# Splitting a weight load, a two-pass first tile, a fourth output buffer and moved final waits in a fused layer kernel

## The chip, the cores and the metric

The kernel runs on one core of a Trainium2 chip. The metric is the device time of one execution in microseconds (us); smaller is better. Executions of the same kernel still spread by 0.4 to 1.8 us. Wherever a difference is below 1 us, I therefore also look into the trace of one execution of each kernel and compare stages, not totals.

The span in a trace is about 1.7 us shorter than the time of the same execution. All times inside a profile are from the start of that span.

## The reference

A transformer layer on 2048 tokens of width 512, in bfloat16: layer norm, then attention with 32 heads of 16 over the 8 earlier positions at stride 2, and beside it a gated feed-forward part.

```python
x = A_x                                     # [1, 2048, 512]
xn = _layernorm(x, axis=-1)
return x + _A_ref(xn, A_wqkv, A_wo) + _B_ref(xn, B_w_gate, B_w_up, B_w_down)

# _A_ref:  qkv = xn @ wqkv   (512 x 1536: Wq, Wk, Wv side by side)
#          ... softmax over the 8 positions ..., then  o @ wo
# _B_ref:  h = gelu(xn @ w_gate) * (xn @ w_up)  (512 x 1376),  then  h @ w_down
```

Both branches read the normalised x. The order at the start: x arrives, its statistics are taken, it is normalised and transposed (`xnT`), and then TensorE projects it with Wq and after that with Wk. At the end the last row tile of the sum is added and stored.

## The kernel before

The kernel is built from a list of tasks; a scheduler orders them on each engine and works out the semaphore waits. Five places matter.

All loads go through SyncE's queue, in this order at the start: two loads of x, Wq, a tile of x, Wk, another tile of x, and later Wv and the weights of the feed-forward part. Wq and Wk are one load of 512 KB each:

```python
for i, nm in enumerate(("q", "k", "v")):
    def mk(i=i):
        return lambda e: e.dma_start(
            Wqkv[:, :, i * 512:(i + 1) * 512],
            A_wqkv[:, i * 512:(i + 1) * 512].rearrange("(k p) n -> p k n", p=128))
    t_w = G.task("sp", "ld_w" + nm, 0, mk(), wr=[(I_wq, nm)],
                 prio=(-958, -957.5, -898)[i], nbytes=512 * 1024)
```

Before the first real matmul, TensorE runs filler matmuls on zeros (`wsrc`) to get its full clock. The first Q tile has four groups `g` of columns, each summed over four row blocks `kt` of Wq, and starts in two pieces, groups 0 and 1, then 2 and 3:

```python
WARM = cfg.get("WARM", ([512] * 8 + [128], [512, 128]))
# ... (cut)
for g in gs:                                  # (0, 1), then (2, 3)
    for kt in range(4):
        ins = e.matmul(
            PS[:, 512 * it.slot + 128 * g:512 * it.slot + 128 * g + 128],
            lhsT=Wqkv[:, kt, which * 512 + g * 128:which * 512 + (g + 1) * 128],
            rhs=xnT[:, itx.slot, kt, t * 128:(t + 1) * 128],
            start=(kt == 0), stop=(kt == 3))
# ... (cut)
chain(warm_tasks[:len(WARM[0])] + ["tpx0_0"] + warm_tasks[len(WARM[0]):] +
      ["mma0_0", "tpx0_1", "mmt0_0", "mmt0_1", "mmt1_0", "tpx1_0", ...])   # order on TensorE
```

In that chain `tpx` are transposes of x, `mma0_0` and `mmt0_0` the first Q tile, `mmt0_1` the second Q tile, and `mmt1_0` the first tile that needs Wk.

At the end VectorE adds a PSUM tile to x into one of `NOB = 3` output buffers, and SyncE stores it. The program's last instructions on SyncE are waits for the totals of all 24 DMA semaphores:

```python
for t in self.order[eng_name]:
    # ... (cut)
    for (s, v) in t.waits:
        e.wait_ge(s, v)
    ins = t.emit(e)
    ins.then_inc(t.sem, 16 if eng_name == "sp" else 1)
if eng_name == "sp":
    for (s, tot) in self.dma_totals:
        e.wait_ge(s, tot)
```

## Time and profile before

| | before |
|---|---|
| median of 3 runs | 194.91 us (194.59 to 194.97) |
| span of the profiled execution | 192.8 us |
| TensorE busy | 186.6 us, 97% |
| first projection starts | 6.29 us |
| TensorE's last signal | 190.33 us |
| landing of the last store | 192.21 us |
| end | 192.79 us |

TensorE is the bound in the middle and has next to no gaps there. So a gain can only come from the 6.3 us before the first projection, from a wait soon after it, or from the 2.5 us behind the last matmul.

### The profile page before, as it was taken

The numbers are of one execution on the slowest core, as the hardware profiler recorded it, in microseconds if no ns is written. First come the engines' busy times: TensorE is split into PE (matmuls) and PEld (weight loads), VectorE is DVE, ScalarE is ACT, GpSimd is POOL, SyncE is SP. The second block draws the span as 40 slices with busy tenths as digits, with TensorE's granted clock in tenths as the row PEclk, the third lists the DMA queues.
The fourth block names the chain that finished last, engine by engine and source line by source line (L and its number), as shares of the span: only waits on it lengthen the run. The fifth ranks groups of instructions, "written<-read, shape, count | busy, mean of one in ns | idle before, by whom it ended". The sixth has DMA issues, their size and how long they took to land.

```text
span 192.8 us, 3283 instructions
## 1 busy us (share of the span) xinstructions
PE 186.6 (97%) x1239; PEld 92.0 (48%) x1256; DVE 152.4 (79%) x240; ACT 106.1 (55%) x177; POOL 15.7 (8%) x31
## 2 busy tenths in 40 slices
PE   6899999999999999999999999999999999999994
PEld 2794444444444444444444444444444444444484
DVE  5799999999997965999995599998996199912132
ACT  5688565696896766712466587328276720058000
POOL 7010011110931020000000000000000000000000
PEclk9999999999999999999999999999999999999999
DMA  4999997899564014965401596420250496130121
GB/s 143 353 397 332 307 172 139 229 235 219 146 131 106 0 40 134 239 140 161 146 19 28 143 237 157 130 77 0 69 139 13 113 233 165 36 112 0 51 72 46
DMA packets 34800, 27.04 MB, mean 140 GB/s; under 512 B 11264, under 2 KB 33248, under 8 KB 34784
## 3 DMA queue, kind: packets, MB, share of 16 engines
q1 hardware_dynamic: 34784, 26.83, 56.2%
q8 instruction: 10, 0.16, 0.3%
q14 instruction: 6, 0.05, 0.1%
HBM read 19.99 MB, written 5.26 MB: 131 GB/s over the span
## 4 chain that ended last, share of the span: by engine, by line
PE 93%; DMA 4%; issue 1%; SPq 0%; DVE 0%; DVEq 0%
PE PS L1395 36%; PE PS L1474 18%; PE PS L1152 18%; PE PS L1470 7%; PE PS L1098 4%; PE PS L1363 4%; PE PS L1236 4%; DMA Wqkv<-in_A_wqkv_dram 2%; PE PS L1430 2%; DMA out_dram<-OB 1%; PE PS L1229 1%; SPq L923 0%; DVE OB L1494 0%; PE PS L1040 0%; DVEq L558 0%
## 5 line engine op out<-in xcount | busy, mean ns | idle before, releaser
L1412 ACT ACTIVATE UU<-PS 128x512 bf16<-128x512 f32 x40 | 24.1, 603 | 35.7 <-PE PS L1395 35.7
L1474 PE MATMUL PS<-Wd,HT 128*128 128x512 bf16 (+2 forms) x207 | 41.1, 345 | 0.1
L1395 PE MATMUL PS<-xnT,Wu 128*128 128x512 bf16 x155 | 39.8, 379 | 0.7 <-issue 0.5
L1395 PE MATMUL PS<-xnT,Wg 128*128 128x512 bf16 x155 | 39.2, 379 | 0.5 <-ACT OT L1375 0.2
L1206 DVE TENSOR_TENSOR UNI<-QT,KT 128x2048 bf16<-128x2048 bf16 x32 | 37.0, 1219 | 2.6 <-PE PS L1363 2.5
L1152 PE MATMUL PS<-xnT,Wqkv 128*128 128x512 bf16 x156 | 35.3, 379 | 0.2
L1417 DVE TENSOR_TENSOR HT<-GG,UU 128x512 bf16<-128x512 bf16 x40 | 16.6, 419 | 20.1 <-ACT UU L1412 20.0
L1405 ACT ACTIVATE GG<-PS 128x512 bf16<-128x512 f32 x40 | 23.7, 601 | 15.0 <-PE PS L1395 12.2
L1474 PEld LDWEIGHTS PS<-Wd,HT 128*128 128x128 bf16 x209 | 19.6, 98 | 18.6
L1395 PEld LDWEIGHTS PS<-xnT,Wu 128*128 128x128 bf16 x160 | 15.3, 98 | 19.6 <-issue 1.3
L1395 PEld LDWEIGHTS PS<-xnT,Wg 128*128 128x128 bf16 x160 | 15.5, 98 | 19.3 <-ACT OT L1375 0.4
L1152 PEld LDWEIGHTS PS<-xnT,Wqkv 128*128 128x128 bf16 x160 | 15.6, 98 | 18.6
L1343 DVE TENSOR_TENSOR BS<-BS,PT 128x2048 bf16<-128x2048 bf16 x16 | 19.6, 1224 | 0.4
L1343 DVE TENSOR_TENSOR UNI<-BS,PT 128x2048 bf16<-128x2048 bf16 x16 | 19.5, 1218 | 0.0
L1494 DVE TENSOR_TENSOR OB<-PS,XR 128x512 bf16<-128x512 f32 (+2 forms) x19 | 11.2, 603 | 10.0 <-PE PS L1474 9.4
L1470 PE MATMUL PS<-Wo,OT 128*128 128x512 bf16 (+2 forms) x76 | 16.9, 345 | 0.0
L1176 ACT ACTIVATE VT<-PS 128x512 bf16<-128x512 f32 x16 | 9.6, 597 | 4.4 <-PE PS L1152 4.4
L1375 ACT ACTIVATE OT<-PS 128x512 bf16<-128x512 f32 x16 | 8.3, 602 | 5.0 <-PE PS L1363 5.0
L940 DVE BATCH_NORM_STATS2 st<-XIN 128x6 f32<-128x512 bf16 x15 | 10.1, 686 | 0.9 <-DMA XIN<-in_A_x_dram 0.9
L1470 PEld LDWEIGHTS PS<-Wo,OT 128*128 128x128 bf16 x76 | 7.2, 98 | 7.0
L1192 POOL COPY KT<-KT 128x64 bf16<-128x64 bf16 x3 | 8.0, 2655 | 17.5 <-ACT KT L1169 16.1
L1162 ACT ACTIVATE QT<-PS 128x512 bf16<-128x512 f32 x12 | 7.2, 597 | 3.1 <-PE PS L1152 3.1
(73 smaller groups left out, 151.9 us busy)
## 6 DMA issues: line engine op xcount, KB each, us to landing
BS<-vt_scratch SPq DMA_DIRECT2D x64, 128.5 KB, 3.5
vt_scratch<-VT SPq DMA_DIRECT2D x16, 128.0 KB
XR<-in_A_x_dram SPq DMA_DIRECT2D x16, 128.0 KB, 2.2
out_dram<-OB SPq DMA_DIRECT2D x14, 128.0 KB, 1.9
Wqkv<-in_A_wqkv_dram SPq DMA_DIRECT2D x3, 512.0 KB
XIN<-in_A_x_dram SPq DMA_DIRECT2D x6, 256.0 KB, 4.4
Wg<-in_B_w_gate_dram SPq DMA_DIRECT2D x1, 1280.0 KB
Wu<-in_B_w_up_dram SPq DMA_DIRECT2D x1, 1280.0 KB
```

The costliest lines, as they stand in the source:

```text
L940: return lambda e: e.bn_stats(out=st[:, t, :], in_=XIN[:, it.slot, t2, :])
L1152: ins = e.matmul(PS[:, 512 * it.slot:512 * it.slot + HWD], lhsT=lhsT, rhs=xnT[:, itx.slot, kt, c0:c0 + HWD], start=(kt == 0), stop=(kt == 3))
L1176: return lambda e: e.activation(out=VT[:, ito.slot, 0:HWD], in_=PS[:, 512 * it.slot:512 * it.slot + HWD], func=ACTF.Identity)
L1206: return lambda e: e.tensor_tensor(out=UNI[:, it.slot, :, :], in0=bass.AP(QT, (itq.slot * 4 + g) * 512, [[NQT * 4 * 512, 128], [0, 4], [1, ...
L1343: return lambda e: e.tensor_tensor(out=dst(), in0=bass.AP(BS, it.slot * 4 * 514 + o, [[NBS * 4 * 514, 128], [514, 4], [128, 4], [1, 128]]) ...
L1395: ins = e.matmul(PS[0:M, 512 * it.slot:512 * it.slot + 512], lhsT=Wx[:, kt, j * 128:j * 128 + M], rhs=xnT[:, itx.slot, kt, :], start=(kt = ...
L1405: return lambda e: e.activation(out=GG[0:M, ito.slot, :], in_=PS[0:M, 512 * it.slot:512 * it.slot + 512], func=ACTF.Gelu_apprx_tanh)
L1412: return lambda e: e.activation(out=UU[0:M, ito.slot, :], in_=PS[0:M, 512 * it.slot:512 * it.slot + 512], func=ACTF.Identity)
L1417: return lambda e: e.tensor_tensor(out=HT[0:M, ito.slot, j, :], in0=GG[0:M, ig.slot, :], in1=UU[0:M, iu.slot, :], op=ALU.mult)
L1470: ins = e.matmul(PS[:, 512 * it.slot:512 * it.slot + CW], lhsT=OT[:, ito.slot, dq, ti * 128:(ti + 1) * 128], rhs=Wo[:, dq, c0:c1], start=( ...
L1474: ins = e.matmul(PS[:, 512 * it.slot:512 * it.slot + CW], lhsT=HT[:, ith.slot, j, ti * 128:(ti + 1) * 128], rhs=Wd[:, j, c0:c1], start=Fal ...
L1494: return lambda e: e.tensor_tensor(out=OB[:, ito.slot, 0:CW], in0=PS[:, 512 * it.slot:512 * it.slot + CW], in1=XR[:, itx.slot, c0:c1], op= ...
```

## The change

The intent: let the first projection start when half of Wq is there; keep the last addition from waiting for an old store; do the bookkeeping waits ahead of the last store and not behind it. The diff, cut to its core:

```diff
@@ emit_engine @@
                 e.wait_ge(s, v)
+            if eng_name == "sp" and t is self.order["sp"][-1]:
+                late = self.order["sp"][-5:]
+                for (s, tot) in self.dma_totals:
+                    if not any(q.sem is s for q in late):
+                        e.wait_ge(s, tot)
             ins = t.emit(e)
@@
         if eng_name == "sp":
-            for (s, tot) in self.dma_totals:
-                e.wait_ge(s, tot)
+            for q in self.order["sp"][-5:]:
+                e.wait_ge(q.sem, q.val)
@@ buffers @@
-    NOB = cfg.get("NOB", 3)
+    NOB = cfg.get("NOB", 4)
-        junk = sb("junk", [128, 512], BF)          # its two uses now write XR slot 0
@@ memset of wsrc ordered first on VectorE (cut); fillers @@
-        WARM = cfg.get("WARM", ([512] * 8 + [128], [512, 128]))
+        WARM = cfg.get("WARM", ([512] * 8 + [128], [128]))
@@ loads @@
+            if nm == "q":
+                for h in range(2):
+                    def mk_h(h=h):
+                        return lambda e: e.dma_start(
+                            Wqkv[:, 2 * h:2 * h + 2, 0:512],
+                            A_wqkv[256 * h:256 * h + 256, 0:512].rearrange("(k p) n -> p k n", p=128))
+                    t_w = G.task("sp", "ld_wq%d" % h, 0, mk_h(), wr=[(I_wq, "q%d" % h)], prio=-958 + 0.1 * h,
+                                 nbytes=256 * 1024)
+            else:
+                t_w = G.task("sp", "ld_w" + nm, 0, mk(), wr=[(I_wq, nm)],
+                             prio=(0, -957.5, -898)[i], nbytes=512 * 1024)
@@ first Q tile @@
-                                for g in gs:
-                                    for kt in range(4):
+                                for g in range(4):
+                                    for kt in ks:
-                                            start=(kt == 0), stop=(kt == 3))
+                                            start=(kt == 0 and not part), stop=(kt == 3 and (g == 3 or not part)))
@@
-                            t_mm = G.task("pe", "mma0_0", 8 * 0.0563, mk_mm((0, 1)), rd=mrd, wr=[it_mm],
-                                          prio=-100, mode="f")
-                            gs = (2, 3)
+                            def mk_z(it=it_mm):
+                                return lambda e: e.matmul(PS[:, 512 * it.slot:512 * it.slot + 512], lhsT=wsrc[:, 0:128],
+                                                          rhs=wsrc[:, :], start=True, stop=False)
+                            t_mm = G.task("pe", "zq0", d_mm(512), mk_z(), rd=[I_wsrc], wr=[it_mm], prio=-400, mode="f")
+                            t_mm = G.task("pe", "mma0_0", 8 * 0.0563, mk_mm((0, 1)), rd=mrd[:1] + [(I_wq, "q0")],
+                                          wr=[it_mm], prio=-100, mode="f")
+                            ks = (2, 3)
@@ order on TensorE @@
-                chain(warm_tasks[:len(WARM[0])] + ["tpx0_0"] + warm_tasks[len(WARM[0]):] +
+                chain(warm_tasks[:len(WARM[0])] + ["tpx0_0", "zq0"] + warm_tasks[len(WARM[0]):] +
```

More of the change, by code (lines that the diff above doesn't have):

```diff
@@ L814, in bass_parallel_sum__sliding_local_dilated__glu_gated_geglu__prompt_kernel @@
         PC2 = cfg.get("PC2", 8)
-        G.task("dve", "c_wsrc", 0.25, lambda e: e.memset(wsrc[:, :], 0.0), wr=[I_wsrc], prio=PC - 1)
+        t_mem = []
+        t_mem.append(G.task("dve", "c_wsrc", 0.25, lambda e: e.memset(wsrc[:, :], 0.0), wr=[I_wsrc], prio=PC - 1))
         G.task("pool", "c_ones", 0.2, lambda e: e.memset(cf[:, :], 1.0), wr=[I_cf], prio=PC)
@@ L838, in bass_parallel_sum__sliding_local_dilated__glu_gated_geglu__prompt_kernel @@
             out=E4f[:, :], in0=cf[:, 0:32], in1=cf[:, 32:64], op=ALU.add), rd=[I_cf], wr=[I_E4f], prio=PC2)
-        G.task("dve", "c_wdz", 0.25, lambda e: e.memset(Wd[0:32, 10, :], 0.0), wr=[(I_wd, 2)], prio=PC + 1)
-        G.task("dve", "c_htz", 0.4, lambda e: e.memset(HT[0:32, :, 10, :], 0.0), wr=[I_htz], prio=PC + 2)
+        t_mem.append(G.task("dve", "c_wdz", 0.25, lambda e: e.memset(Wd[0:32, 10, :], 0.0), wr=[(I_wd, 2)], prio=PC + 1))
+        t_mem.append(G.task("dve", "c_htz", 0.4, lambda e: e.memset(HT[0:32, :, 10, :], 0.0), wr=[I_htz], prio=PC + 2))
+        G.order_after(t_mem[1], t_mem[0])
+        G.order_after(t_mem[2], t_mem[0])
         G.task("pool", "c_e4b", 0.3, lambda e: e.tensor_tensor(
@@ L877, in mk @@
                     A_wqkv[:, i * 512:(i + 1) * 512].rearrange("(k p) n -> p k n", p=128))
-            t_w = G.task("sp", "ld_w" + nm, 0, mk(), wr=[(I_wq, nm)],
-                         prio=(-958, -957.5, -898)[i], nbytes=512 * 1024)
+            if nm == "q":
[9 more added lines that the diff above has]
+                             prio=(0, -957.5, -898)[i], nbytes=512 * 1024)
             t_ld["w" + nm] = t_w
@@ L942, in bass_parallel_sum__sliding_local_dilated__glu_gated_geglu__prompt_kernel @@
                     for (nm, dur, kw, rd, wr) in (
-                            ("sx1", 0.55, dict(out=junk[:, :], func=ACTF.Identity, accum_out=sums[:, 0:1]),
+                            ("sx1", 0.55, dict(out=XR[:, 0, :], func=ACTF.Identity, accum_out=sums[:, 0:1]),
                              [], [I_junk, (I_sums, 0)]),
@@ L946, in bass_parallel_sum__sliding_local_dilated__glu_gated_geglu__prompt_kernel @@
                                                 scale=-1.0 / D), [(I_sums, 0)], [(I_sums, 1)]),
-                            ("sxx1", 0.55, dict(out=junk[:, :], func=ACTF.Square, bias=sums[:, 1:2],
+                            ("sxx1", 0.55, dict(out=XR[:, 0, :], func=ACTF.Square, bias=sums[:, 1:2],
                                                 accum_out=sums[:, 2:3]), [(I_sums, 1)], [I_junk, (I_sums, 2)]),
@@ L1091, in bass_parallel_sum__sliding_local_dilated__glu_gated_geglu__prompt_kernel, with mk_mm @@
                         it_mm = Item("mmt%d_%d" % (which, t), P_ps, "qkv")
-                        def mk_mm(gs, which=which, t=t, it=it_mm, itx=XTI[0]):
+                        def mk_mm(ks, which=which, t=t, it=it_mm, itx=XTI[0]):
                             def f(e):
                                 ins = None
-                                for g in gs:
-                                    for kt in range(4):
+                                part = len(ks) < 4
+                                for g in range(4):
+                                    for kt in ks:
                                         ins = e.matmul(
@@ L1101, in f @@
                                             rhs=xnT[:, itx.slot, kt, t * 128:(t + 1) * 128],
-                                            start=(kt == 0), stop=(kt == 3))
+                                            start=(kt == 0 and not part), stop=(kt == 3 and (g == 3 or not part)))
                                 return ins
                             return f
-                        mrd = ([(XTI[0], (t // 2, t % 2)), (I_wq, "qk"[which])]
-                               + ([(XTI[0], ("y", 0, t))] if t < 2 else []))
-                        gs = (0, 1, 2, 3)
+                        mrd = ([(XTI[0], (t // 2, t % 2))] + ([(XTI[0], ("y", 0, t))] if t < 2 else [])
+                               + ([(I_wq, "k")] if which else [(I_wq, "q0"), (I_wq, "q1")]))
+                        ks = (0, 1, 2, 3)
                         if t == 0 and which == 0:
-                            t_mm = G.task("pe", "mma0_0", 8 * 0.0563, mk_mm((0, 1)), rd=mrd, wr=[it_mm],
-                                          prio=-100, mode="f")
+                            def mk_z(it=it_mm):
+                                return lambda e: e.matmul(PS[:, 512 * it.slot:512 * it.slot + 512], lhsT=wsrc[:, 0:128],
+                                                          rhs=wsrc[:, :], start=True, stop=False)
+                            t_mm = G.task("pe", "zq0", d_mm(512), mk_z(), rd=[I_wsrc], wr=[it_mm], prio=-400, mode="f")
+                            t_mm.urgent = True
+                            t_of["zq0"] = t_mm
+                            t_mm = G.task("pe", "mma0_0", 8 * 0.0563, mk_mm((0, 1)), rd=mrd[:1] + [(I_wq, "q0")],
+                                          wr=[it_mm], prio=-100, mode="f")
                             t_mm.urgent = True
                             t_of["mma0_0"] = t_mm
-                            gs = (2, 3)
-                        t_mm = G.task("pe", "mmt%d_%d" % (which, t), 4 * len(gs) * 0.0563, mk_mm(gs), rd=mrd,
+                            ks = (2, 3)
+                        t_mm = G.task("pe", "mmt%d_%d" % (which, t), 4 * len(ks) * 0.0563, mk_mm(ks), rd=mrd,
                                       wr=[it_mm], prio=-100 + t, mode="f")
@@ L1156, in bass_parallel_sum__sliding_local_dilated__glu_gated_geglu__prompt_kernel @@
                         t_mm = G.task("pe", "mm%d_%d_%d_%d" % (b, which, g, hf), d_mm(HWD, 4), mk_mm(),
-                               rd=xparts + [(I_wq, "qkv"[which])],
+                               rd=xparts + ([(I_wq, "kv"[which - 1])] if which else [(I_wq, "q0"), (I_wq, "q1")]),
                                wr=[it_mm], prio=hb + 10 + (1 if which == 2 else 0), mode="f",
```

## The prediction

> **What bounds the kernel now.** I read the page's engine shares, then TensorE's waits, then the chain of work that ended last, then the timelines of the first 8 and the last 4 us.
>
> ```profile
> PE 186.6 (97%) x1239; PEld 92.0 (48%) x1256; DVE 152.4 (79%) x240; ACT 106.1 (55%) x177; POOL 15.7 (8%) x31
> ...
> PE 93%; DMA 4%; issue 1%; SPq 0%; DVE 0%; DVEq 0%
> ```
>
> TensorE is busy for 97% of the span and carries 93% of the chain. Its waits (us in total, times, longest) are few:
>
> ```profile
> PE PS L866 <- DVE wsrc L815: 1.5, 1, 1.5
> PE PS L1098 <- DMA Wqkv<-in_A_wqkv_dram: 0.7, 1, 0.7
> PE PS L1395 <- issue: 0.6, 4, 0.2
> PE PS L1395 <- ACT OT L1375: 0.3, 2, 0.2
> ```
>
> The first two lie ahead of the first real matmul; the others are pauses of 0.16 us that follow the narrow-tile matmuls. I added up the trace's gaps between matmuls from 6.29 us (first projection) to 190.32 us (modelled end of the last): 1.56 us in 184, none above 0.16. **So the middle has nothing to give.** What is left is 6.3 us before TensorE runs unbroken and 2.5 us after it stops. The chain (start us, us, what) names a DMA at both ends:
>
> ```profile
> 1.71 4.44 DMA Wqkv<-in_A_wqkv_dram
> 6.15 0.14 issue
> 6.29 0.61 PE PS L1098 x8
> ...
> 187.56 2.85 DMA out_dram<-OB
> 190.41 0.02 issue
> 190.44 0.29 DVE OB L1494
> ```
>
> The load of Wq releases the first projection; a store out of the output buffer releases the last addition. For each the question is what else ends just behind it.
>
> **What the Trainium skill says.** "DMA: Bandwidth & Descriptors", section "Why a DMA increments its semaphore by 16 and not by 1": sixteen engines finish independently, and only the full 16 means that all data is there. The landing records agree: of Wq's sixteen, fourteen are in by 5.69 us and the last two at 6.02 and 6.15; of the store issued at 187.56, fifteen are in by 189.09 and the last at 190.415. "Perfetto Trace Analysis", section "Identifying Dependency Chains": an instruction with many waits may have EventSemaphore instructions inserted before it. This build does that, two waits each: the 24 final waits became twelve such instructions and a wait on the branch. "TensorE: Matmul & The Clock Gate", section "What's actually happening": full clock comes after a busy, free-running window of some 3.4 us. Here the fillers start at 1.51 us and full clock is granted at 4.74, 3.23 us later and before the first transposes at 4.95. "PSUM — Partial Sum Buffer", section "The four PSUM rules": a matmul with the start flag clears the whole bank's written-bits, so four accumulations interleaved in one bank can't each start with it. That is why the change starts the bank with one 512-wide zero matmul and adds onto it; no trace here shows the rule itself.
>
> **Part 1, Wq in two loads and the first Q tile in two passes.** Wq is 512 KB, behind two x loads that land at 2.83 and 3.37 us; so it moves between some 3.4 and 6.15. Its first half should land about half way, near 5.0 us (estimate from these landings). Then Wq no longer holds the first matmul, but ScalarE's copy of transposed x does:
>
> ```profile
> 5.52 0.30 ACT L972 ACTIVATE sq<-mv,eps 128x1 bf16<-128x1 bf16 x1
> 5.72 0.36 ACT L1060 ACTIVATE xnT<-PS 128x256 bf16<-128x256 bf16 x1
> ```
>
> It signals at 6.09. For the second x tile the same handover, from ScalarE's signal at 7.55 to the first matmul at 7.597, takes 0.047 us, so the first matmul can start at 6.14 in place of 6.29: **0.15 us, not the 0.67 that the wait shows**, because ScalarE's statistics of tile 1 and this copy are a chain that the change leaves alone. What follows moves with it: eight matmuls (8 x 0.056 = 0.44) to 6.58, then the transposes of tile 1, whose input VectorE finishes at 6.40; its copies and the next Q tile, 7.60 to 7.45. The second half of Wq is needed at about 6.81 and should land where Wq did, at 6.15. Wk is issued one issue (0.45) later, but it waits in a stream that is limited by bytes, not by issue: it landed at 8.00, and is needed at 8.35. All later weights have 2 us or more. From 7.60 on TensorE runs unbroken, so 0.15 reaches the end of the matmuls.
>
> **Part 2, the zero matmul and the fillers.** It replaces a 512-wide filler one for one: 0. The memset of the fillers' source becomes VectorE's first, 0.27 us earlier, so fillers start near 1.24 and end near 4.77. The transposes wait for VectorE (4.54 + 0.35 = 4.89) and don't move: 0, unless the clock window falls badly.
>
> **Part 3, fourth output buffer.** TensorE signalled the last group at 190.33. In the addition before, VectorE's wait began at 189.52 and the addition at 189.59, 0.066 later; without the store, 190.36 + 0.066 = 190.425 in place of 190.439. **Worth 0.014 us in this execution**: the late sixteenth landing and TensorE came together.
>
> **Part 4, the final waits.** The timelines have the last two stores (start us, us), and the view of one line the twelve wait instructions (ns min/median/max, first and last start):
>
> ```profile
> 189.91 0.33 SPq L1501 DMA_DIRECT2D out_dram<-OB  x1
> ...
> 190.76 0.33 SPq L1501 DMA_DIRECT2D out_dram<-OB  x1
> ```
>
> ```profile
> L564 SPq EVENT_SEMAPHORE  x12: 17/28/539, 191.1 to 192.3; - x12
> ```
>
> They begin at 191.14 and come every 0.061 us. The tenth (191.69) holds the last store's count, sits 0.54 us until the landing at 192.207, and two more follow before the branch at 192.39. In the changed program's instruction order ten wait instructions stand ahead of the last store, whose own wait for VectorE stays on the store, and behind it are two, the second with its count. So the branch comes 0.056 us behind the landing in place of 0.183: 0.13 gained. But the ten now run between the last two stores: the earlier issue ends at 190.24, they start at 190.29 and end at 190.29 + 9 x 0.061 + 0.03 = 190.87, and the store can go at 190.90 in place of 190.76: **0.14 lost. The tail nets about zero**, and part 3 is hidden behind it.
>
> **Part 5, the order in the middle.** The build counts the same 838 instructions on TensorE. In the third quarter a gate and an up group move from between the output tiles to behind them, and ScalarE does the exponential with both table loads ahead of a GELU. Output tiles then follow each other at 15 x 0.216 = 3.24 us over two PSUM banks, each freed by an addition of 0.69 us. The order can only lose, since nothing was lost before; I expect 0.
>
> Sum on the profiled execution: -0.15 + 0.01 = -0.14 us.
>
> **The rivals.** (a) The tail as intended: if waits that are met already cost less ahead of a store than the 0.061 after one, or order doesn't matter, the end is 0.13 sooner and the time 194.6. For: VectorE's 0.29 us addition leaves SyncE idle there; against: ten times 0.061 is more than the 0.52 us between the two issues. (b) Late landings are worse in unprofiled runs. The median of 194.91 is 0.41 above the profiled 194.50 and the three runs spread by 0.38. If that is stragglers of Wq or of the store, the change takes out most of it: 194.3 to 194.5. For: the waits sit on a sixteenth landing at both ends; against: no profile shows such a run. (c) A new stall in the middle, VectorE late with freeing a bank, or Wk late: up to 0.3, so 195.1. Against: the slack above. (d) The clock window: earlier fillers could bring full clock sooner where it came late, up to 0.27.
>
> **Range and chances.** From 194.91: -0.14 for the mechanism gives 194.77; half weight to (a) and (b), some 0.17, gives 194.6. Run spread of 0.4 and (c) make the range 194.1 to 195.0. 2% is 3.9 us, more than either end holds in all, so within 2% is nearly sure.
>
> **What would show it.** Right: first projection at 6.12 to 6.18 with ScalarE's copy as releaser; Wq gone from the chain; the last matmul at 190.17; some 0.6 us of wait instructions between the last two stores, and the last store issued about 0.65 behind the one before. Wrong: a first projection much before 6.1; a last store right on VectorE's signal; TensorE gaps beyond 1.6 us in the middle; a difference over 0.5 us.

## The result, and the profile after

| | before | after |
|---|---|---|
| median of 6 runs | 194.78 us (194.42 to 194.97) | 195.08 us (194.66 to 196.06) |
| ratio, with 95% interval | | 1.0025 (1.000 to 1.005) |
| span of the profiled execution | 192.8 us | 193.3 us |

A ratio here is the mean time of one kernel's runs over that of the other's runs of the same rounds, so it isn't quite the ratio of the medians beside it. The time is 0.3 us over the one before where 0.14 under it was expected from the mechanism.

The page after, engine shares and chain:

```profile
PE 187.7 (97%) x1239; PEld 92.6 (48%) x1256; DVE 152.4 (79%) x240; ACT 106.1 (55%) x177; POOL 9.6 (5%) x31
...
PE 93%; DMA 3%; SPq 1%; issue 1%; DVE 0%; DVEq 0%
```

A DMA still holds 3% of the chain. The chain itself (start us, us, what) says which one:

```profile
3.21 5.76 DMA Wqkv<-in_A_wqkv_dram
8.96 0.05 issue
9.01 1.07 PE PS L1115 x16
...
190.85 0.03 issue
190.88 0.02 DVEq L558
190.90 0.04 issue
190.94 0.29 DVE OB L1517
```

Before, the load in the chain was Wq, landing at 6.15, and the store into an output buffer stood ahead of the last addition. Both are gone, as planned. In their place stands **another weight load, issued at 3.21 and landed at 8.96: Wk**. TensorE's timeline (start us, us from first to last, engine, line, ..., idle before and its releaser) shows the start. Before:

```profile
6.29 0.61 PE L1098 MATMUL PS<-xnT,Wqkv 128*128 128x128 bf16 x8 [0.67 <-DMA Wqkv<-in_A_wqkv_dram]
6.73 0.39 PE L1040 MATMUL PS<-ident,XIN 128*128 128x128 bf16 x4
6.96 2.60 PE L1098 MATMUL PS<-xnT,Wqkv 128*128 128x128 bf16 x40
```

After:

```profile
6.08 0.91 PE L1115 MATMUL PS<-xnT,Wqkv 128*128 128x128 bf16 x8
6.83 0.39 PE L1056 MATMUL PS<-ident,XIN 128*128 128x128 bf16 x4
7.05 1.71 PE L1115 MATMUL PS<-xnT,Wqkv 128*128 128x128 bf16 x24
9.01 1.07 PE L1115 MATMUL PS<-xnT,Wqkv 128*128 128x128 bf16 x16 [0.25 <-DMA Wqkv<-in_A_wqkv_dram]
```

Two things are to be seen. The eight matmuls of the first pass start earlier but take 0.91 in place of 0.61, because full clock came only at 6.72 in this execution. And a run of 40 matmuls became 24 and 16 with a hole between them. The 0.25 counts only from the modelled end of the matmul before; from start to start the hole is larger, as the table of stages shows.

I cut both spans into stages at instructions that both kernels have (us). "Again" is a second profile of the same, unaltered kernel, taken as an experiment below. ScalarE's signal is the end of its instruction. A group of matmuls counts from its first weight load, which starts 0.004 to 0.054 ahead of the first matmul in the timelines.

| stage | before | before again | after | after again |
|---|---|---|---|---|
| start to ScalarE's signal for the first xnT | 6.082 | 6.063 | 6.026 | 6.167 |
| from there to the first projection | 0.177 | 0.312 | 0.051 | 0.051 |
| to the transposes of tile 1 (0.41 at full clock) | 0.421 | 0.420 | 0.697 | 0.408 |
| to the first Wk matmul | 1.767 | 1.766 | **2.230** | 1.766 |
| to the third group of transposes | 0.893 | 0.894 | 0.854 | 0.894 |
| to TensorE's last signal | 180.991 | 180.990 | 180.990 | 180.990 |
| to the end | 2.461 | 2.660 | 2.501 | 2.498 |
| sum | 192.79 | 193.11 | 193.35 | 192.77 |

**The middle is identical to a nanosecond or two.** From before to after, the 0.56 us that the span grew are: -0.06 for ScalarE's signal, -0.13 at the first projection, +0.28 for the cold clock, +0.46 - 0.04 for Wk (the stage behind a wait for Wk is up to 0.04 shorter, so a wait of 0.46 costs 0.42), +0.04 at the tail. The rest of this document asks which of these terms belong to the change and which to chance.

Where do Wk's bytes get held up? In the view of the DMA queue between 4 and 8 us the row "GB/s" has 40 slices of 0.1 us. Before, then after:

```profile
GB/s 246 307 369 369 389 389 379 358 389 369 379 399 379 359 379 420 348 410 389 358 338 379 369 379 389 348 328 338 317 318 287 328 338 358 358 369 348 338 338 369
```

```profile
GB/s 297 348 379 338 358 358 317 307 287 277 328 215 113 123 133 154 195 195 184 184 195 215 195 225 276 348 297 307 307 379 341 283 309 328 277 220 261 348 317 267
```

Before, the stream runs at 287 to 420 from 4.1 us on. After, it falls to 113 to 225 from about 5.1 to 6.4 us, when Wq is nearly in and a 128 KB tile of x and Wk are next. This is the **trough** that the experiments look for. Between 5 and 6 us it is 382 GB/s before and 182 after.

The kernel before has such a trough as well, only earlier: between 3 and 4 us, ahead of Wq, which stands behind two 128 KB loads of x. Before, then after (columns: stretch, us, busy share of PE, PEld, DVE, ACT, POOL with counts, granted clock, DMA share, GB/s):

```profile
3.00:4.00 1.00, 1.00 (x3) 0.30 (x2) 0.93 (x3) 0.60 (x2) 0.78 (x5) 1.00 0.59 131
```

```profile
3.00:4.00 1.00, 1.00 (x4) 0.38 (x3) 0.93 (x3) 0.66 (x3) 0.78 (x5) 1.00 0.78 219
```

So the split doesn't make a slow stretch out of nothing: it shortens the one ahead of Wq, and one stands ahead of Wk in its place.

The tail went as worked out: the waits (count: ns min/median/max, first and last start us) stand ahead of the last store, and two remain behind it.

```profile
L563 SPq EVENT_SEMAPHORE  x10: 17/28/28, 190.8 to 191.4; - x10
...
L569 SPq EVENT_SEMAPHORE  x2: 28/28/28, 191.9 to 192.9; - x2
```

The last addition ended at 191.23, and the last store was issued at 191.42, behind the tenth wait.

### The profile page after: what moved, and what is told of

It reads as the page before. It is cut to its first block, busy times and chain, and to the rows that moved or that the text cites. A ratio compares the mean times of both kernels' runs of the same rounds, so it can differ in the third digit from the quotient of the medians.

```text
span 193.3 us, 3282 instructions
## 1 busy us (share of the span) xinstructions
PE 187.7 (97%) x1239; PEld 92.6 (48%) x1256; DVE 152.4 (79%) x240; ACT 106.1 (55%) x177; POOL 9.6 (5%) x31
## 4 chain that ended last, share of the span: by engine, by line
PE 93%; DMA 3%; SPq 1%; issue 1%; DVE 0%; DVEq 0%
PE PS L1418 36%; PE PS L1497 20%; PE PS L1175 18%; PE PS L1493 7%; PE PS L1386 4%; PE PS L1259 4%; DMA Wqkv<-in_A_wqkv_dram 3%; PE PS L1115 3%; PE PS L1453 2%; PE PS L1252 1%; SPq L939 1%; SPq L888 0%; PE PS L1056 0%; DVE OB L1517 0%; DVEq L558 0%
## 5 line engine op out<-in xcount | busy, mean ns | idle before, releaser
L1192 ACT ACTIVATE KT<-PS 128x512 bf16<-128x512 f32 x12 | 7.2, 598 | 2.9 <-PE PS L1175 2.9
```

## The experiments

Theories before the runs. **A**: Wk is late because it is issued one issue later (3.21 in place of 2.74). **B**: Wk is late because of what stands ahead of it in the queue: a load behind small loads starts slowly. **C**: the 0.3 us is chance, namely the phase of the clock window and late landings. Each run below was timed in 5 rounds and has a profile. The three sets ran on three chips: the two repeats, one load and waits at the end on the first; Wk first, waits earlier, Wk in two and four loads on the second; the rest on the third. "Wait for Wk" is the time from the first weight load of the second Q tile to that of the first Wk matmul, less the 0.854 that it takes when nothing holds it; up to 0.04 of it comes back in the next stage. Every run was correct.

Beside timed medians stand the range of 6 runs and the ratio to the kernel before of the same rounds (its medians were 194.93, 194.86 and 194.90 in the three sets).

### The same kernels once more

No edit. **The changed kernel again:**

> The changed kernel, unaltered, for a second profile. Its first profile had Wk landing at 8.96 us (8.00 before) with a 0.42 us wait of TensorE for it, full clock granted only at 6.72 us (4.74 before), and 0.19 us of final waits between VectorE's last signal and the last store. Theory 1 (Wk is late because it is issued one issue later, into a stream that runs dry): Wk lands at 8.7 us or later again, and TensorE waits 0.2 us or more again. Rival (one unlucky execution): Wk at 8.0 to 8.4, no wait. The clock grant should differ from 6.72 if the window runs freely (anywhere from 4 to 7.2). The final waits should delay the last store by 0.15 to 0.2 us again, as nothing in them is chance. Time 195.0 to 195.3 under theory 1, 194.6 under the rival.

Measured: 194.91 (194.57 to 195.65), ratio 1.0009 (0.9986 to 1.0033). Its profile is the last column of the table above: full clock at 4.94, Wk landed at 8.32, no wait for it. The timeline of TensorE:

```profile
6.22 0.62 PE L1115 MATMUL PS<-xnT,Wqkv 128*128 128x128 bf16 x8 [0.52 <-ACT xnT L1076]
6.68 0.39 PE L1056 MATMUL PS<-ident,XIN 128*128 128x128 bf16 x4
6.90 2.60 PE L1115 MATMUL PS<-xnT,Wqkv 128*128 128x128 bf16 x40
```

So the same program can run the start without the cold matmuls and without the hole. The trough was there (212 GB/s between 5 and 6 us), yet Wk landed just before it was needed. The copy of ScalarE came 0.14 later than in the first profile, which is as much as the whole predicted gain.

**The kernel before again:**

> The kernel before, unaltered, for a second profile and as a null control of the timing. Theory 1: Wk at 7.9 to 8.2 us, no wait for it, first projection at 6.2 to 6.3 released by Wq. Rival (chance): Wk somewhere between 8.0 and 9.0. If the clock window runs freely, the grant is elsewhere than 4.74. Ratio 1.000, interval within 0.25%.

Measured: 194.87 (194.59 to 194.97), ratio 0.9997 (0.9978 to 1.0017). In its profile Wq landed at 6.27, and the first projection started 0.312 after ScalarE's signal. The end of its chain:

```profile
187.68 3.06 DMA out_dram<-OB
190.74 0.02 issue
190.76 0.29 DVE OB L1494
```

Here the last addition really waited for the store to free its buffer: it started 0.313 after TensorE's signal, not 0.108 as in the first profile. **With three buffers the wait was thus 0.014, 0.22 and, in a third profile (the split only in the kernel before), 0**, where the prediction read 0.014 from one profile.

The late landing itself isn't chance. In all 14 profiles the last of this store's sixteen landings came 0.94 to 1.84 us behind the fifteenth, and the DMA packets in the traces name what held it: one 16 KB packet of queue q8 (called "instruction" on the page) starts 0.5 to 0.8 us after the store's issue and takes 0.95 to 1.58 us; the store's packets that are left start within 0.015 us of its end, and the sixteenth landing follows 0.94 to 1.10 us after that end. What varies is how long this packet takes. If the same landings had met three buffers, the last addition would have waited 0 to 0.53 in the eleven profiles with four, 0.22 on average (an estimate from these landings and TensorE's signals). No run moves the packet.

What follows from the pair: theory C is right that single profiles differ by 0.3 to 0.6, and the change's own gain has to be found stage by stage.

### Undo the split only

```diff
-                for h in range(2): ...                                # two loads of 256 rows
+                t_w = G.task("sp", "ld_wq", 0, mk(), wr=[(I_wq, "q0"), (I_wq, "q1")], prio=-958, nbytes=512 * 1024)
```

> The changed kernel with Wq in one load again; zero matmul, two passes, fourth buffer and moved waits stay. Theory 1: Wk is issued at 2.74 us again and lands at about 8.0, TensorE does not wait for it; the first projection goes back to about 6.26, held by Wq. Net against the changed kernel: 0.15 us lost at the first projection, 0.4 gained at Wk, so about 0.25 us faster, 194.7 to 194.9. Rival (Wk late by chance): no systematic gain, 0.15 us slower than the changed kernel.

Measured: 194.58 (194.46 to 195.14), ratio 0.9989 (0.9968 to 1.0009). Window view, 5 to 6 us (columns as above):

```profile
5.00:6.00 1.00, 0.83 (x6) 0.50 (x6) 0.69 (x3) 0.94 (x5) 0.00 (x0) 1.00 1.09 378
```

The trough is gone: 378 GB/s against 182. Wk landed at 7.51, and Wq as one load landed at 5.64, so the first projection still started 0.051 after ScalarE's signal. This says that the split isn't needed for the early start in an execution without stragglers, and that it goes together with the trough. Issue order and load size are both restored here, so A and B are not yet told apart.

### The split only, in the kernel before

```diff
+                for h in range(2): ...     # Wq in two loads; all its readers wait for both
```

> The kernel before with only Wq's load split in two; the first Q tile still waits for both halves, no other part of the change. If the split alone makes the slow second of DMA: 100 to 230 GB/s between 5 and 6 us (355 to 382 without the split), Wk complete at 8.3 to 9.0, waits of TensorE for it of 0 to 0.5, while the first projection goes at 6.12 to 6.2 as in the changed kernel, since both halves land before 5.8. Rival (it needs the other parts, such as the first VectorE order or the scratch target): 355 GB/s or more, Wk at 8.0.

Measured: 195.06 (194.41 to 195.48), ratio 0.9998 (0.9969 to 1.0028).

```profile
5.00:6.00 1.00, 0.63 (x6) 0.29 (x6) 0.70 (x3) 0.94 (x5) 0.00 (x0) 1.00 0.51 124
```

The split alone brings the trough ahead of Wk (124 GB/s) and a later Wk (8.31; TensorE waited 0.04, which the next stage gave back). Neither the zero matmul, nor the fillers' order, nor the waits have a part in it.

### Wk issued first

```diff
-                             prio=(0, -957.5, -898)[i], nbytes=512 * 1024)
+                             prio=(0, -957.85, -898)[i], nbytes=512 * 1024)
```

This puts Wk's issue at 2.71, where the kernel before has it (2.74), with the two halves of Wq still ahead of it, and the tile of x that stood between them behind it.

> The changed kernel with Wk issued right behind the two halves of Wq, ahead of the third x tile: at 2.70 us, as in the kernel before (2.74), in place of 3.21. Three profiles with Wq in two loads have Wk landing at 8.96, 8.32 and 8.54, and DMA at 100 to 212 GB/s between 5 and 6 us; three with one load have 8.00, 8.23 and 7.51, and 355 to 382. Theory A (a big load needs a fixed lead from issue to full flow, and the half of Wq ahead of it is too short to cover it): Wk lands 0.5 sooner than in the changed kernel, 7.8 to 8.2, no wait of TensorE for it, time some 0.2 us less. Theory B (after small loads a 512 KB load starts slowly whatever its issue): the slow second only moves, Wk at 8.2 to 8.6 and waits of 0 to 0.2. The third x tile comes later, at 8 us or so, and under either theory could hold VectorE's statistics at 7.3 us and cost what Wk gives.

Measured: 196.09 (195.04 to 196.69), ratio 1.0053 (1.0027 to 1.0079).

```profile
5.00:6.00 1.00, 1.00 (x6) 0.52 (x6) 0.70 (x3) 0.94 (x5) 0.00 (x0) 1.00 0.70 137
```

```profile
PE PS L1056 <- DVE XIN L1030: 1.1, 1, 1.1
PE PS L1115 <- DMA Wqkv<-in_A_wqkv_dram: 0.2, 1, 0.2
```

The trough stayed (137 GB/s), and Wk, issued half a microsecond sooner, landed at 8.95, as late as in the changed kernel (8.96), with a wait of 0.43. **Theory A fell here**, which expected 7.8 to 8.2; B's figure of 8.2 to 8.6 was missed too. The run is slower for its own reason: the third x tile, now behind Wk, landed at 9.28, and TensorE waited another 1.1 for VectorE's normalised x of it.

### One load of Wq, but Wk's issue held back

```diff
+            if t.name == "ld_wk":            # wait for a GpSimd instruction that ends near 3.1 us
+                for q in self.order["pool"]:
+                    if q.name == "c_e4a":
+                        e.wait_ge(q.sem, q.val)
```

on top of the one load: the reverse of the run before.

> The changed kernel with Wq in one load, and Wk held back by a wait of SyncE for a GpSimd instruction that ends at about 3.1 us: Wk is issued at 3.15 to 3.3, as late as in the changed kernel, but behind one 512 KB load. If the late issue were the cause, Wk lands at 8.3 to 9.0 with a slow second. If the small loads ahead are the cause (as issuing Wk first and four loads speak for): no slow second, 345 GB/s or more between 5 and 6 us, Wk at 7.5 to 8.2, no wait.

Measured: 194.87 (194.62 to 195.08), ratio 0.999 (0.9962 to 1.0017). Wk was issued at 3.14, nearly as late as in the changed kernel.

```profile
5.00:6.00 1.00, 0.97 (x6) 0.56 (x6) 0.68 (x4) 0.94 (x5) 0.00 (x0) 1.00 1.12 346
```

No trough: 346 GB/s. But Wk landed at 8.57, where 7.5 to 8.2 was expected without one, with fourteen of its sixteen parts in by 8.11 and two stragglers, and TensorE waited 0.23. So late issue doesn't make the trough; that it has a small part in the landing of Wk can't be excluded from one profile.

### Wk in two loads as well

```diff
+            elif nm == "k":
+                for h in range(2): ...       # Wqkv[:, 2*h:2*h+2, 512:1024] <- 256 rows; readers wait for both
```

> The changed kernel with Wk in two loads of 256 rows as well, second half issued at about 3.7 us. Theory A (lead time from issue): the first half starts as late as Wk did, the second is issued 0.47 later still, Wk complete at 8.4 to 9.0, waits of 0.1 to 0.4 us and DMA at 100 to 212 GB/s between 5 and 6 us. Theory B (a 512 KB load starts slowly, a 256 KB one doesn't): no slow second, 330 GB/s or more between 5 and 6, Wk complete by 8.0, no wait.

Measured: 194.75 (194.53 to 195.81), ratio 1.0000 (0.9978 to 1.0023). 221 GB/s between 5 and 6 us; the second half of Wk, issued at 3.70, landed at 8.43; wait 0.07. No clear gain over the changed kernel: a smaller Wk load doesn't take the trough away, though this is the shallowest one. The form of B in which a 256 KB load doesn't start slowly fell here.

### Wq in four loads

```diff
-                for h in range(2): ...
+                for h in range(4):
+                    def mk_h(h=h):
+                        return lambda e: e.dma_start(Wqkv[:, h, 0:512], A_wqkv[128 * h:128 * h + 128, 0:512])
```

> A stronger dose: Wq in four loads of 128 rows, so Wk is issued two issues later again, at about 4.15 us. Theory A (lead time from issue): Wk lands another 0.8 to 1.0 us later, at 9.2 to 9.9, and TensorE waits 0.8 us or more; time 0.5 to 0.8 us over the changed kernel. Theory B (512 KB load after small ones): Wk at 8.3 to 9.0 as with two loads, waits of 0 to 0.4. If Wq's last quarter itself is late (needed at 6.85), the second half of the first Q tile waits too.

Measured: 195.45 (194.91 to 196.13), ratio 1.003 (1.0008 to 1.0052).

```profile
5.00:6.00 1.00, 1.00 (x6) 0.55 (x6) 0.68 (x4) 0.94 (x5) 0.00 (x0) 1.00 0.74 192
```

Wk was issued at 4.09, 0.88 later than in the changed kernel, and landed at 8.91 against 8.96; wait 0.49. If issue time decided, it would have come some 0.9 later than the 8.31 to 9.11 of the five profiles with halves; it came within them. It is the clearest single number against A. The interval is all above 1, so in timed runs this kernel is slower than the kernel before.

### Wq in 128 and 384 rows

```diff
-                            Wqkv[:, 2 * h:2 * h + 2, 0:512],
-                            A_wqkv[256 * h:256 * h + 256, 0:512]...
+                            Wqkv[:, h:1 + 3 * h, 0:512],
+                            A_wqkv[128 * h:128 + 384 * h, 0:512]...       # first pass waits for both
```

Again two loads, and Wk issued at 3.20, but the second load of Wq is 384 KB.

> The changed kernel with Wq in a load of 128 rows and one of 384; the first pass waits for both. If what matters is a big load right ahead of Wk (its data still moving while Wk's descriptors are handed out), 384 KB should do nearly as well as 512: 300 GB/s or more between 5 and 6 us, Wk at 7.8 to 8.3. If it is enough that Wq comes in two pieces: 100 to 230 GB/s, Wk at 8.3 to 9.0.

Measured: 194.73 (194.46 to 195.81), ratio 0.9989 (0.9957 to 1.0021).

```profile
5.00:6.00 1.00, 1.00 (x6) 0.56 (x6) 0.68 (x4) 0.94 (x5) 0.00 (x0) 1.00 1.04 323
```

323 GB/s and no wait for Wk, which landed at 8.43. So it isn't the number of loads either: **two loads with a large one last keep the stream full, two of 256 KB don't** (one profile of this kernel; a 128 KB tile of x stands between Wq and Wk in either). This kernel has its slow stretch earlier again, 130 GB/s between 3 and 4 us. The price was that Wq's last part landed at 6.26 and held the first projection by 0.14. The tail of this profile is 0.28 longer than the changed kernel's: the issue of the third store from the end took 0.82 us in place of 0.33 (0.50 and 0.71 in the two profiles of the kernel before). I don't know why.

### Final waits back at the end

```diff
-            if eng_name == "sp" and t is self.order["sp"][-1]: ...
-            for q in self.order["sp"][-5:]: ...
+            for (s, tot) in self.dma_totals:
+                e.wait_ge(s, tot)
```

> The changed kernel with all final waits back behind the last store. My theory: the last store goes 0.02 us after VectorE's signal in place of 0.19 to 0.20, and two wait instructions more (0.13 us) stand between landing and branch: 0.05 us faster, not to be seen in the times but in the trace. Rival (the moved waits are worth what they take off the end): 0.13 us slower with the last store issued no earlier.

Measured: 194.82 (194.71 to 195.28), ratio 1.0002 (0.998 to 1.0024). From TensorE's last signal to the end: 2.494 with the waits behind the last store, 2.498 and 2.501 with them directly ahead of it.

```profile
L564 SPq EVENT_SEMAPHORE  x12: 17/28/589, 191.2 to 192.4; - x12
```

The last store went at 190.836, 0.41 after TensorE's signal (0.57 in the changed kernel), but the branch came 0.24 after the landing in place of 0.084. **Moving the waits there nets zero**, as predicted (this run's own 0.05 isn't to be seen).

### Final waits two stores earlier

```diff
-            if eng_name == "sp" and t is self.order["sp"][-1]:
+            if eng_name == "sp" and t is self.order["sp"][-3]:
```

> The changed kernel with the nineteen early final waits ahead of the third-last store in place of the last. There SyncE is idle for over 1 us, so the ten wait instructions should end before VectorE signals. My theory: the last store goes 0.02 us after VectorE's signal (0.19 to 0.20 in the changed kernel), the branch stays 0.08 us behind the landing (0.18 with all waits at the end), and from TensorE's last signal to the end of the span it takes 2.50 - 0.17 = 2.33 us (2.49 to 2.51 in four profiles with the waits in either place). Rival (waits already met cost nothing in front of a store, and something else delays the last store): still 2.5.

Measured: 195.03 (194.48 to 195.26), ratio 0.9999 (0.9981 to 1.0017).

```profile
L563 SPq EVENT_SEMAPHORE  x10: 17/28/28, 188.6 to 189.2; - x10
```

Now the ten waits stand in idle time of SyncE and are over by 189.2, nearly 2 us before the last addition starts at 191.09. The stage from TensorE's last signal to the end is **2.348, 0.15 shorter** than in the changed kernel. The timed median doesn't show it, because this kernel still has the trough (90 GB/s); its profile waited 0.54 for Wk.

### The two findings together

The changed kernel with Wq in one load and the waits ahead of the third store from the end.

```diff
+                t_w = G.task("sp", "ld_wq", 0, mk(), wr=[(I_wq, "q0"), (I_wq, "q1")], prio=-958, nbytes=512 * 1024)
-            if eng_name == "sp" and t is self.order["sp"][-1]:
+            if eng_name == "sp" and t is self.order["sp"][-3]:
```

> A version that should beat both: the changed kernel with Wq in one load and the early final waits ahead of the third-last store. From the traces so far: Wk not waited for, first projection 6.14 to 6.25, TensorE's 180.99 us from the third transposes to its last signal as in all others, and 2.35 us from there to the end in place of 2.50 (2.46 and 2.66 in the two profiles of the kernel before). Time 0.2 to 0.4 us below the kernel before, ratio 0.998 to 0.999.

Measured: 194.41 (194.23 to 194.78), ratio 0.997 (0.994 to 1.000). No trough (379 GB/s), no wait for Wk (landed 7.72), a tail of 2.350. This is the lowest median and below both kernels'; its interval just reaches 1, so a gain of 0.3% over the kernel before is likely, not proved. Against the changed kernel the trace names two parts: the wait ahead of the last store that is gone, and a Wk that is in time. Against the kernel before, where Wk was in time, they are the tail (2.461 and 2.660 there) and a first projection that didn't wait for Wq (0.051 against 0.177 and 0.312), which in this kernel comes from Wq's landing at 5.87 and not from a split.

### All profiles side by side

| kernel | Wk issued | GB/s, 5 to 6 us | Wk landed | wait for Wk | full clock at | ratio |
|---|---|---|---|---|---|---|
| before; again | 2.74; 2.74 | 382; 354 | 8.00; 8.23 | 0; 0 | 4.74; 5.96 | 1; 0.9997 |
| one load | 2.75 | 378 | 7.51 | 0 | 5.39 | 0.9989 |
| one load, waits earlier | 2.74 | 379 | 7.72 | 0 | 5.08 | 0.997 |
| one load, Wk held | 3.14 | 346 | 8.57 | 0.23 | 5.85 | 0.999 |
| 128 + 384 rows | 3.20 | 323 | 8.43 | 0 | 6.17 | 0.9989 |
| **changed; again** | 3.21; 3.22 | **182; 212** | 8.96; 8.32 | 0.46; 0 | 6.72; 4.94 | 1.0025; 1.0009 |
| waits at the end | 3.21 | 136 | 8.54 | 0.22 | 5.21 | 1.0002 |
| waits earlier | 3.21 | 90 | 9.11 | 0.54 | 6.79 | 0.9999 |
| split in the kernel before | 3.22 | 124 | 8.31 | 0.04 | about 4.2 | 0.9998 |
| Wk in two as well | 3.22, 3.70 | 221 | 8.43 | 0.07 | 5.06 | 1.0000 |
| Wk first | 2.71 | 137 | 8.95 | 0.43 | 6.70 | 1.0053 |
| four loads | 4.09 | 192 | 8.91 | 0.49 | 6.45 | 1.003 |

The column GB/s falls into two classes with nothing between 221 and 323, and the size of the largest load of Wq, over or up to 256 KB, is what separates them. The issue time doesn't: 2.71 has a trough, 3.14 and 3.20 have none. Between 3 and 4 us the same two classes stand the other way round: 96 to 131 GB/s in the six profiles with Wq in a load of 384 or 512 KB, 219 to 250 in the eight with halves or quarters. Each chip of the first and third set has both classes, so it isn't the chip.

## Why the prediction was right or wrong

**Wrong: the step on Wk.** It said: "Wk is issued one issue (0.45) later, but it waits in a stream that is limited by bytes, not by issue: it landed at 8.00, and is needed at 8.35." The issue was later as told, and this alone made no trough (346 GB/s with Wk held), though that one profile waited 0.23, with two stragglers. What failed is the other half: it was read from a stream with Wq in one load. With Wq in halves it isn't limited by bytes: it falls to 90 to 212 GB/s for a microsecond in the five profiles with Wq in halves, Wk in one load and the changed kernel's order of loads. There Wk landed 8.31 to 9.11, and TensorE waited 0.46, 0, 0.22, 0.54 and 0.04: **0.25 on average**, of which 0.22 was lost, as the next stage gives up to 0.04 back. I had carried over a landing from a stream whose make-up the change alters. My rival (c), "or Wk late: up to 0.3, so 195.1", is what happened, and I had put it aside with "the slack above", that is, with the step that failed.

**Mis-sized: the gain at the first projection.** The mechanism was right: with the split, ScalarE's copy releases the matmul, 0.051 after its signal in all eight profiles with Wq in halves or quarters (0.045 to 0.047 by the prediction's own measure, from the semaphore to the matmul; predicted 0.047). But what it gains was read from one execution. In the five profiles with Wq in one load the same handover took 0.177, 0.312, 0.051, 0.051 and 0.051. So the gain is 0.126, 0.261 or nothing, 0.08 on average, not 0.15: it is the gain only when the last of Wq's sixteen landings is late. For the execution that it was read from, 0.15 was right (0.126, and 0.013 in the next stage). The average pools two kernels: both profiles with a late Wq are of the kernel before, the three without are of the changed kernel with one load, and whether that is chance isn't shown. Net of Wk, part 1 costs some 0.15 by these averages of five profiles.

**Left out: the phase of the clock.** I called the earlier fillers 0 "unless the clock window falls badly", and it did in the profiled run after: 0.28 on its first eight matmuls. Over the 14 profiles full clock came from 4.2 (read from the fillers' pace in the one trace without a record of it) to 6.8, and the starts of the fillers differ only by 0.26. I take it for chance and no part of the change's cost, since the changed kernel, unaltered, had it at 6.72 once and at 4.94 once. That isn't shown: cold matmuls behind the first projection fell in four of the eleven profiles with the earlier fillers and in none of the three with the later ones, which is too few to tell. And rival (d), that earlier fillers bring full clock sooner, has nothing for it.

**Right: the zero matmul, the middle, the tail.** From the third transposes to TensorE's last signal all kernels take 180.99 us, except Wk first (180.95); part 5 is 0, as said. The tail nets zero: the last store stood 0.667 behind the one before (predicted "about 0.65"), and it was held 0.19 after VectorE was done. Rival (a), met waits costing less ahead of a store, is refuted: they come every 0.061 there too. The fourth buffer's mechanism was right, and its size was one draw: 0 to 0.22 in three profiles, up to 0.53 by the estimate from the other landings; that is the part of rival (b) that I saw.

**So the sum** was to be -0.14 and comes out, from these averages, as -0.08 + 0.22 at the start. The tail gives -0.04 (2.461, 2.660 and 2.496 with three buffers against some 2.50) or, by the estimate from all 14 landings, some -0.15 (a mean wait of 0.19, less the 0.04 by which the changed kernel's tail is longer than one with three buffers and no wait). Together that is about 0 to +0.1, the cold clock left out. The intervals of the changed kernel's two ratios, 1.0025 and 1.0009, don't exclude it, but the 1.0025 (some +0.5) isn't explained by it: no timed run shows its stages.

**Open.** Why a large load behind loads of 256 KB or less starts slowly isn't shown, for Wk as for Wq; the runs show only when it does. The four profiles with full clock at 6.4 or later and a trough are also the ones with the latest Wk (8.91 to 9.11), the others have 8.31 to 8.54. Whether one makes the other, or both follow the moment of the start, I couldn't tell apart (three of the four are of one set, on one chip, where the fourth profile had 5.06 and 8.43). And as no timed run shows its stages, the 0.25 is a mean of profiled executions only.

## What to carry to other kernels

Before splitting a load to free the first reader, look at the load behind it: its landing time belongs to the stream as it was, and slack read from it is void once the sizes change, so compare GB/s in that stretch before and after. A wait shown at 0.67 was worth 0.14 in its own profile, because ScalarE's copy ended close before Wq landed, and 0.08 on average; a second profile of the same kernel is the cheapest way to see which waits vary. A landing that is late in every profile has a cause that the packet records may show. Bookkeeping waits that are already met should go where their engine is idle, two stores earlier, and not directly ahead of the last store.

## What the Trainium skill lacked or had wrong

- On no page: the first large load behind small ones starts slowly. Ahead of Wq in a load of 384 or 512 KB, behind 128 KB loads of x, SyncE's queue moved 96 to 131 GB/s between 3 and 4 us; ahead of Wk, with Wq in loads of at most 256 KB, it moved 90 to 221 GB/s between 5 and 6 us, against 323 to 382 GB/s with a Wq load of 384 or 512 KB. The page "DMA: Bandwidth & Descriptors" would be the place. The cause is open.
- "DMA: Bandwidth & Descriptors", section "Why a DMA increments its semaphore by 16 and not by 1", is right that the engines finish independently, but gives no size for it: the last of Wq's sixteen landings came 0.46 and 0.60 us behind the fourteenth and the fifteenth in the two profiles of the kernel before, and that of one store 0.94 to 1.84 us behind the fifteenth in all 14.
- On no page: what an instruction packet costs a data transfer. One 16 KB packet of queue q8 took 0.95 to 1.58 us in the 14 profiles, and the rest of that store's packets came only at its end. "Runtime: NRT & Kernel Launch" would be the place.
- On no page: a wait instruction whose semaphores are already met costs SyncE 0.061 us from start to start, whether it stands ahead of a store or behind it; with ten of them ahead a store went 0.19 us after VectorE's end in place of 0.03.
- "TensorE: Matmul & The Clock Gate", section "What's actually happening", is borne out in that the moment scatters from run to run, but not in the size of the scatter: the page has plus or minus 500 ns, and here full clock came between 4.9 and 6.8 us in the eleven profiles with fillers from 1.25 us. It doesn't say how busy a window must be. In the first profile after the change full clock came at 6.72, so by the page's 3.4 us (an estimate from that page) the window before it ended near 3.3 with fillers from 1.25 on: some 60% busy, and it wasn't granted.
